# One value tile of an attention decode kernel loaded as its even rows and then eight 8-row transfers

## Chip, cores, metric

One core of one Trainium2 chip. The metric is device time in microseconds (us) of one execution. Repeats of the kernel before agree within 0.05%.

## The reference, cut to what matters

One decode step: layer norm, attention of 4 new tokens over a cache, output projection, residual, then a gated MLP with residual.

```python
B, Sq, D = 4, 1, 512;  H, Sk, Dh = 32, 8192, 128
scores = einsum("bhqd,bhkd->bhqk", q, k_cache) * Dh ** -0.5
p = softmax(scores);  o = einsum("bhqk,bhkd->bhqd", p, v_cache)
h = x + o.reshape(B, Sq, H * Dh) @ wo          # then h + MLP(layernorm(h))
```

k_cache and v_cache hold 268 MB each in bfloat16 and are read once; everything else is small. Loads are the whole cost.

## The kernel before

The cache passes through a ring of 4 buffers of 4 MiB, 128 partitions of 32 KiB. A tile is two heads of keys or of values; 64 tiles of each. SyncE issues every load, each as soon as the former tile in its buffer has been used. Row p of a tile (32 KiB, contiguous in HBM) goes to partition p.

```python
ring = SB("ring", [128, NS, TW], BF16)                     # NS = 4, TW = 16384
...
def kv_src(t, cache):                                      # [128 rows, 32 KiB each]
    h = 2 * t
    return cache[h // H, h % H:h % H + 2, :, :].rearrange("h (p r) d -> (h p) (r d)", p=64)
...
def load(it):
    kind, t = it
    slot = slot_of.get(it)
    ...                                                    # the last tiles are cut in pieces
    uses[slot] += 1
    sem, val = s_slot[slot], 16 * uses[slot]
    if kind == "k":
        dst, src = ringv(slot), kv_src(t, A_k_cache)
    elif kind == "v":
        dst, src = ringv(slot), kv_src(t, A_v_cache)
    ...
    return [(lambda e: e.dma_start(dst, src).then_inc(sem, 16), sem, val)]
```

VectorE transposes key tiles, TensorE makes scores and the products with the value tiles; both wait for the tile's semaphore. At the end a tail of pieces (output projection, MLP weights, last value tile) is issued, with the last two full tiles interleaved.

## Time and profile before

| | before |
|---|---|
| time, median | 1295.27 us (4 runs, 1295.11 to 1295.41) |
| DMA rate in the stream | 427 to 434 GB/s |
| key tile, issue to landing | 29.7 us |
| value tile, issue to landing | 33.9 us |
| VectorE busy | 636.9 us (49%) |
| TensorE matmul busy | 494.7 us (38%) |

The page of the kernel before: the DMA busy share and rate in 40 slices of the span, the packet counts, the queue, the chain that ended last, and two lines of the issues (count, KB each, us to landing). q1 is SyncE's queue, q8 and q14 fetch instructions.

```profile
DMA  9999999999999999999999999999999999999998
GB/s 405 432 428 433 433 427 433 431 430 434 427 431 432 429 431 432 432 428 433 432 430 429 433 429 431 431 432 431 431 429 432 431 429 434 430 430 431 428 382 322
DMA packets 26069, 551.46 MB, mean 426 GB/s; under 512 B 2340, under 2 KB 8232, under 8 KB 9256
...
q1 hardware_dynamic: 26016, 550.78, 99.5%
q8 instruction: 38, 0.62, 0.2%
q14 instruction: 7, 0.06, 0.0%
...
DMA 80%; PE 12%; SPq 4%; DVE 3%; issue 0%; ACT 0%
...
ring<-in_A_k_cache_dram SPq DMA_DIRECT2D x64, 4096.0 KB, 29.7
ring<-in_A_v_cache_dram SPq DMA_DIRECT2D x63, 4096.0 KB, 33.9
```

The DMA engines are busy throughout, and a tile takes 9.7 us of stream but lands 30 us or more after its issue: some three tiles always stand in the queue. No compute engine is near full. The kernel is bound by its 16 DMA engines.

Stages of the kernel before (us; then busy time and instruction count of TensorE matmuls, TensorE weight loads, VectorE, ScalarE and GpSimd; TensorE clock; DMA share; GB/s). The middle ones are those where the change will act.

```profile
600.00:690.00 90.00, 33.88 (x310) 11.78 (x314) 49.13 (x50) 3.67 (x6) 0.00 (x0) 0.58 1.00 431
692.00:696.00 4.00, 1.51 (x21) 0.41 (x20) 0.71 (x1) 2.61 (x5) 0.00 (x0) 0.93 1.05 451
698.00:718.00 20.00, 8.73 (x74) 3.88 (x74) 10.39 (x11) 0.00 (x0) 0.00 (x0) 0.59 1.01 432
730.00:830.00 100.00, 36.78 (x357) 12.88 (x349) 48.12 (x47) 3.67 (x6) 0.00 (x0) 0.61 1.00 430
```

In a stage of 4 us the rate is rough (451 GB/s; a packet of 32 KiB may count wholly in one stage); over 20 us it is 432 GB/s, as everywhere.

The trace also has a record of every DMA packet. It says nothing about which engine moved it, but each engine moves its packets back to back (eight of 1.216 us make the 9.72 us from one tile to the next), and each transfer ends with one 4-byte semaphore packet per engine that took part (16 for a whole tile, 4 for the 4-row load of x). So the finishing times of the 16 engines can be read tile by tile. Times of packets are counted here, as in the profile views, from the start of the span. A 32 KiB packet takes 1.216 us (median), eight per engine and tile. For the tile that ends from 720 us on:

```
before, 16 semaphore packets of one tile, us after the first at 720.8:
0 0.31 0.43 0.51 0.58 0.69 1.00 | 3.38 3.40 3.43 3.51 3.99 4.88 5.07 5.26 5.48
```

Seven engines are ahead of nine. The gaps come from instruction fetches, as the prediction tells: after a 16 KiB fetch one of the 16 finishing times moves back by about 1.55 us (at 593, 634 or 886 us, for example), after one of 8 KiB by 0.97 us.

### The profile page before, as it was taken

Reading aid. Unit: us, or ns where it says so; the run is one execution under the profiler, and the core shown is the slowest. Engines: PE = TensorE matmul, PEld = TensorE weight load, DVE = VectorE, ACT = ScalarE, POOL = GpSimd, SP = SyncE. Lnnn points to the kernel's source line nnn. Section 1 sums busy time; section 2 is a strip of 40 time slices with the busy share of each in tenths; the row PEclk is TensorE's granted clock in tenths of the full one; section 3 lists DMA queues with packets and bytes.
Section 4 is the critical chain, followed back from the end, with each engine's and each line's share of the span. In section 5 each row is a group of like instructions: output and inputs, shape, how many; then the busy total and the mean of one; then the engine's idle time right before and its main releaser. Section 6 shows DMA issues by size and latency. Waiting matters only on the chain.

```text
span 1293.4 us, 10805 instructions
## 1 busy us (share of the span) xinstructions
PE 494.7 (38%) x4867; PEld 183.3 (14%) x4867; DVE 636.9 (49%) x657; ACT 70.7 (5%) x118; POOL 10.7 (1%) x22
## 2 busy tenths in 40 slices
PE   2443334334234244334334334343343343343436
PEld 1011111111011011111111111011111111111114
DVE  5974644545545544635536545545545446445300
ACT  2010100001010010100101010010100101000010
POOL 3000000000000000000000000000000000000000
PEclk8556566566565565565565666665665655665665
DMA  9999999999999999999999999999999999999998
GB/s 405 432 428 433 433 427 433 431 430 434 427 431 432 429 431 432 432 428 433 432 430 429 433 429 431 431 432 431 431 429 432 431 429 434 430 430 431 428 382 322
DMA packets 26069, 551.46 MB, mean 426 GB/s; under 512 B 2340, under 2 KB 8232, under 8 KB 9256
## 3 DMA queue, kind: packets, MB, share of 16 engines
q1 hardware_dynamic: 26016, 550.78, 99.5%
q8 instruction: 38, 0.62, 0.2%
q14 instruction: 7, 0.06, 0.0%
q10 hardware_dynamic: 8, 0.00, 0.0%
HBM read 550.77 MB, written 0.00 MB: 426 GB/s over the span
## 4 chain that ended last, share of the span: by engine, by line
DMA 80%; PE 12%; SPq 4%; DVE 3%; issue 0%; ACT 0%
DMA ring<-in_A_v_cache_dram 76%; PE PS L441 7%; PE PS L417 4%; SPq L222 2%; DMA ring<-in_A_k_cache_dram 2%; DVE kT L399 2%; SPq L238 1%; DMA ring<-in_A_wq_dram 1%; DMA ring<-in_B_w_down_dram 1%; SPq L230 1%; SPq L258 0%; PE PS L332 0%; DVE Lq L376 0%; DVE ring L349 0%; PE PS L359 0%
## 5 line engine op out<-in xcount | busy, mean ns | idle before, releaser
L399 DVE STREAM_TRANSPOSE kT<-ring 128x1024 uint32<-128x1024 uint32 x512 | 587.9, 1209 | 480.9 <-DMA ring<-in_A_k_cache_dram 480.9
L417 PE MATMUL PS<-kT,Lq 128*32 128x512 bf16 x2048 | 241.3, 619 | 570.1 <-DVE kT L399 447.8
L441 PE MATMUL PS<-ring,PTz 128*32 128x512 bf16 x2048 | 215.6, 566 | 205.3 <-DMA ring<-in_A_v_cache_dram 205.3
L417 PEld LDWEIGHTS PS<-kT,Lq 128*32 128x32 bf16 x2048 | 69.0, 136 | 705.4 <-DVE kT L399 481.6
L441 PEld LDWEIGHTS PS<-ring,PTz 128*32 128x32 bf16 x2048 | 64.9, 128 | 323.2 <-DMA ring<-in_A_v_cache_dram 196.8
L476 ACT ACTIVATE negm<-PS 128x1 f32<-128x1 f32 x16 | 2.7, 171 | 1125.1 <-PE PS L472 1125.1
L502 DVE STREAM_TRANSPOSE Et<-Ep 128x512 bf16<-128x512 bf16 x16 | 11.4, 712 | 97.4 <-ACT Ep L498 97.4
L511 ACT ACTIVATE PTz<-Et 64x512 bf16<-64x512 bf16 x32 | 34.0, 1062 | 12.8 <-DVE Et L502 12.5
L516 DVE TENSOR_SCALAR Zs<-PS,rinv 128x512 f32<-128x512 f32 x16 | 11.6, 723 | 37.6 <-PE PS L441 37.6
L523 PE MATMUL PS<-SelZ,Zs 128*128 128x8 f32 x128 | 17.8, 265 | 0.9 <-DVE Zs L516 0.9
L523 PEld LDWEIGHTS PS<-SelZ,Zs 128*128 128x128 f32 x128 | 16.3, 200 | 9.9 <-issue 8.1
L455 DVE TENSOR_REDUCE mx<-PS 128x1 f32<-128x512 f32 x16 | 10.5, 657 | 3.9 <-PE PS L417 3.9
L478 ACT ACTIVATE E_sb<-PS,negm 128x512 bf16<-128x512 f32 x16 | 11.0, 688 | 0.7 <-ACT negm L476 0.2
L498 ACT ACTIVATE Ep<-PS 128x512 bf16<-128x512 f32 x16 | 9.6, 597 | 11.3 <-PE PS L494 11.3
L483 PEld LDWEIGHTS PS<-sig,Gsum 128*128 128x128 f32 x32 | 8.0, 313 | 13.4 <-issue 13.4
L483 PE MATMUL PS<-sig,Gsum 128*128 128x1 f32 x32 | 9.4, 363 | 0.0
L472 PEld LDWEIGHTS PS<-onesf,rowx 1*128 1x128 f32 x32 | 6.8, 265 | 12.5 <-issue 12.5
L472 PE MATMUL PS<-onesf,rowx 1*128 1x1 f32 x32 | 8.2, 323 | 0.0
L494 PE MATMUL PS<-E_sb,Sel 128*32 128x512 bf16 x64 | 7.0, 429 | 1.9 <-ACT E_sb L478 1.3
L349 DVE CAST ring<-PS 128x512 bf16<-128x512 f32 x4 | 2.5, 684 | 9.8 <-PE PS L332 9.8
L528 DVE CAST OT<-PS 128x8 bf16<-128x8 f32 x16 | 2.1, 132 | 9.6 <-PE PS L523 9.6
L332 PE MATMUL PS<-ring,xnT 128*32 128x512 bf16 x32 | 3.5, 615 | 6.6 <-DMA ring<-in_A_wq_dram 6.6
(80 smaller groups left out, 85.4 us busy)
## 6 DMA issues: line engine op xcount, KB each, us to landing
ring<-in_A_k_cache_dram SPq DMA_DIRECT2D x64, 4096.0 KB, 29.7
ring<-in_A_v_cache_dram SPq DMA_DIRECT2D x63, 4096.0 KB, 33.9
ring<-in_A_wq_dram SPq DMA_DIRECT2D x1, 4096.0 KB, 12.3
kT<-in_A_wo_dram SPq DMA_DIRECT2D x8, 512.0 KB, 17.3
ring<-in_A_v_cache_dram SPq DMA_DIRECT2D x1, 2048.0 KB, 18.6
ring<-in_A_v_cache_dram SPq DMA_DIRECT2D x2, 1024.0 KB, 18.2
ring<-in_B_w_gate_dram SPq DMA_DIRECT2D x1, 1792.0 KB, 20.0
ring<-in_B_w_up_dram SPq DMA_DIRECT2D x1, 1792.0 KB, 23.5
```

What stands on the lines that cost most here:

```text
L222: return [(lambda e: e.dma_start(wo_v[:, HW * t:HW * t + HW, :], A_wo.rearrange("(h p) f -> p h f", p=128)[:, HW * t:HW * t + HW, :]).then ...
L230: return e.dma_start(ringv(slot)[:, c0:c1], kv_src(t, A_v_cache)[:, c0:c1]).then_inc(s_piece[i], 16)
L238: return e.dma_start(wd_v[:, t0:t1, :], B_w_down.rearrange("(t p) f -> p t f", p=128)[:, t0:t1, :]).then_inc(s_piece[3 + i], 16)
L399: return e.transpose(kT[:, buf, i * q:(i + 1) * q].bitcast(U32), ringv(src)[:, base + i * q:base + (i + 1) * q].bitcast(U32))
L417: mm = e.matmul(bS[g % 2][32 * j:32 * (j + 1), :], Lq[:, l0:l0 + 32], rhs, start=(s % GS == 0 and v == 0), stop=(s % GS == GS - 1 and v == 3),
L441: mm = e.matmul(bO[g % 2][32 * rq:32 * (rq + 1), :], PTz[:, g % 2, l0:l0 + 32], ringv(slot)[:, r0 * 128:(r0 + 4) * 128], start=(s % GS == ...
L472: p2_of[g] = P("pe", lambda e: e.matmul(bX[:, 0:1], rowx[0:1, :], onesf[0:1, 0:1], start=True, stop=True), [d2b_of[g], c_ones])
L483: L_of[g] = P("pe", lambda e: e.matmul(bX[:, 0:1], Gsum[:, :], sig[:, 0:1], start=True, stop=True), [exp_of[g], a1_of[g], d_g])
L502: et_of[g] = P("dve", lambda e: e.transpose(Et[:, :], Ep[:, :]), [epc_of[g]] + list(ptc_of.get(g - 1, ())))
L511: return e.activation(dst, src, ACT.Copy)
L516: z_of[g] = P("dve", lambda e: e.tensor_scalar(Zs[:, :], bO[g % 2][:, :], rinv[:, g % 2:g % 2 + 1], None, op0=ALU.mult), [pv_of[g * GS + G ...
L523: mm = e.matmul(bX[:, 256:264], Zs[:, 128 * r:128 * (r + 1)], SelZ[:, r, :], start=(r == 0), stop=(r == 3))
```

## The change

Value tile 32 of 64, in the middle, is no longer loaded by one transfer of 128 rows but by nine: the 64 even rows, then 8 transfers of 8 rows that lie 16 apart (1, 17, ..., 113; then 3, 19, ...). The bytes, their places and the final semaphore count are the same. The name LOW8 suggests the intent, which the code does not state: it moves work to eight engines, presumably those that are ahead.

```diff
+        LOW8 = ("v", NT2 // 2)
+        LOW8_PARTS = [slice(0, 127, 2)] + [slice(p, p + 113, 16) for p in range(1, 16, 2)]
+
         def load(it):
             kind, t = it
             slot = slot_of.get(it)
+            if it == LOW8:
+                uses[slot] += len(LOW8_PARTS)
+                ops = []
+                for ps in LOW8_PARTS:
+                    def f(e, ps=ps, sem=s_slot[slot]):
+                        return e.dma_start(ring[ps, slot, :], kv_src(t, A_v_cache)[ps, :]).then_inc(sem, 16)
+                    ops.append((f, s_slot[slot], 16 * uses[slot]))
+                return ops
```

## The prediction

> **What bounds the kernel.** The DMA engines: the 40-slice table has their busy share at 9 in 39 slices, 427 to 434 GB/s until the tail; the stages view gives DMA 1.00 from 60 to 1180 us, VectorE about half. The chain of waits is 76% value-tile transfers. Tiles land about 30 us after issue (29.7 key, 33.9 value: the issue list), so some three tiles of 9.7 us stand in the queue.
>
> The trace's packet records say more. A 4 MiB tile is 128 packets of 32 KiB, median 1.216 us, back to back on 16 engines, 8 each. So the time is the packet sum of the engine furthest behind, and they are not level: for the tile landing near 700 us seven finish within 1.0 us, nine 3.3 to 5.5 us later; at the last key tile nine are 5.35 to 8.66 us behind. The cause is 16 KiB instruction fetches (36 records; about 1.06 us each and a slowed packet, about 1.55 us lost), which visit eight engines in turn; a ninth gets rarer 8 KiB fetches (about 0.97 us lost each) and ends 5.35 us behind.
>
> **What the change does.** Same bytes, same buffer, one tile of 128. The even rows, 64, put 4 packets on each of 16 engines. Each odd transfer has 8 rows. [...] The 4-row load of x has 4 data and 4 semaphore packets[...] +4 x 1.216 = +4.9 us low, -4.9 us high. Eight more semaphore packets per low engine (9 ns each): under 0.1 us. Eight more issues of 0.33 us: hidden by the queue. All waits use the final count.
>
> **On the critical path.** The low engines' surplus stays, since later tiles are balanced and the queue never runs dry. Its cost depends on which engines lag. My reading is that the eight fetch engines are the high half, so the change unloads laggards: they end at most 3.8 us behind instead of 8.66. Low engines end 5 to 6 us behind, but the ninth laggard would be low: 5.35+4.9=10.2. Net 0 to +1.5 us. If laggards are in the low half, the full +4.9. A further risk: [...] odd packets take up to double and the total could rise 10 to 20 us. No packet of this trace tests that.
>
> **Prediction:** 1297 us (+2 us, +0.15%); 80% range 1293 to 1309. Faster by over 2%: 0.005; within 2%: 0.97; slower by over 2%: 0.025.
>
> **What would show it.** 64 odd packets on eight engines near 700 us, of about 1.22 us [...]; the split tile landing 4 to 5 us later against its neighbours; afterwards the finishing spread within a tile changed by about 9.7 us between the halves, kept to the end; tail length, VectorE and TensorE busy times unchanged.
>
> **What would make it wrong.** Engines chosen by partition, not count (0 us); [...] the fast half being the low half without the ninth laggard (up to 3 us faster); gaps of a microsecond per transfer that the queue doesn't hide (+8 us).

The sum came to 0 to +1.5 us net, put as +2 us (1297 us). What stood before "+4 x 1.216" is the author's estimate, from the 4-row load with its 4 semaphore packets, that an 8-row transfer runs on 8 engines, so that eight engines ("low") carry 4+8=12 packets of this tile and the other eight ("high") 4, instead of 8 each. The risk of 10 to 20 us was named outside the sum; it stands as the author's guess.

## More of the kernel before

The chain of waits of the kernel before near the tile in question (start us, us, what):

```profile
672.92 0.02 issue
672.93 34.37 DMA ring<-in_A_v_cache_dram
707.30 0.14 issue
```

The waits for loads (us in total, times, longest us):

```profile
DVE kT L399 <- DMA ring<-in_A_k_cache_dram: 480.9, 60, 11.6
...
PE PS L441 <- DMA ring<-in_A_v_cache_dram: 205.3, 65, 10.5
```

A key tile comes every other tile, about every 19.4 us, and VectorE works about 9 us on it, so waits of some 10 us are normal (11.6 us is the longest); a disturbance of the stream must show as a longer one.

## The result

1310.97 us median of 4 runs (1310.35 to 1313.77), against 1295.27 us for the kernel before: 15.7 us slower. The ratio is 1.0125, 95% interval 1.0108 to 1.0143. Ratios here are the mean time of one kernel's fast runs over the mean of the other's in the same rounds, so not quite the ratio of the medians quoted. That is within 2%, but eight times the forecast +2 us and above the range (up to 1309). The profiled execution was the run of 1313.77 us, the slowest of the four; this matters for the tail below.

The page after:

```profile
DMA  9999999999999999999999999999999999999997
GB/s 405 430 431 432 431 431 431 432 430 432 431 431 431 431 430 431 431 433 430 431 430 273 410 432 431 431 432 432 431 430 431 430 431 431 431 431 432 398 367 303
DMA packets 26133, 551.46 MB, mean 420 GB/s; under 512 B 2404, under 2 KB 8296, under 8 KB 9320
...
q1 hardware_dynamic: 26080, 550.78, 99.2%
```

One slice has fallen to 273 GB/s and the next to 410, while the busy share above it still shows 9: the engines were busy but moved half as much. The packet count rose by 64, all of them tiny (under 512 B): the even rows have the 16 semaphore packets that the whole tile had before, and 8 more transfers have 8 each. So an odd transfer does run on 8 engines.

The same stages after:

```profile
600.00:690.00 90.00, 33.47 (x310) 11.77 (x314) 49.13 (x50) 3.66 (x6) 0.00 (x0) 0.58 1.00 431
692.00:696.00 4.00, 1.85 (x21) 0.63 (x21) 0.71 (x1) 2.27 (x5) 0.00 (x0) 0.86 1.05 451
698.00:718.00 20.00, 2.42 (x18) 0.95 (x18) 9.76 (x10) 0.00 (x0) 0.00 (x0) 0.50 0.99 214
730.00:830.00 100.00, 38.72 (x361) 14.09 (x353) 48.20 (x48) 3.67 (x6) 0.00 (x0) 0.60 1.00 430
```

The even rows, at about 691 to 696 us, still ran at full rate. The 20 us in which the odd transfers ran had 214 GB/s at a DMA share of 0.99. From 730 us on the rate is what it was.

The chain and the waits after (L231 is the new transfer's line; the value tile's matmuls are now L454, the key transposes L412):

```profile
678.22 0.56 SPq L231
678.78 0.05 issue
678.83 47.13 DMA ring<-in_A_v_cache_dram
725.96 0.14 issue
```

```profile
DVE kT L412 <- DMA ring<-in_A_k_cache_dram: 499.0, 60, 27.7
...
PE PS L454 <- DMA ring<-in_A_v_cache_dram: 226.6, 65, 21.1
```

The tile landed at 725.96 us instead of 707.30. The wait of VectorE for keys rose by 18.1 us, with one wait of 27.7 us instead of at most 11.6. Issuing cost nothing that mattered. All nine issues together took 5.98 us of the queue, more than the 0.33 us apiece that was predicted:

```profile
673.41 5.98 SPq L231 DMA_DIRECT2D ring<-in_A_v_cache_dram  x9
```

but that ended 12 us before the first packet of the tile was due. VectorE busy (636.6 us) and TensorE busy (494.1 us) are unchanged.

In the packet records of the profiled run, 192 packets of 32 KiB that started between 696 and 725 us took over 1.35 us ("slow" below), their median 2.40 us. Together they took 216 us more than at 1.216 us each. Over 16 engines this is 13.5 us: most of the loss. The tile has only 64 odd packets. The other two thirds of the slow packets are the neighbouring loads on the same and on the other eight engines: in this phase no engine was fast.

### The profile page after: what moved, and what is told of

It is laid out like the page before. It is cut to its first block, busy times and chain, and to the rows that moved or that the text cites. A ratio compares the mean times of both kernels' runs of the same rounds, so it can differ in the third digit from the quotient of the medians.

```text
span 1311.8 us, 10813 instructions
## 1 busy us (share of the span) xinstructions
PE 494.1 (38%) x4867; PEld 183.4 (14%) x4867; DVE 636.6 (49%) x657; ACT 70.7 (5%) x118; POOL 10.6 (1%) x22
## 4 chain that ended last, share of the span: by engine, by line
DMA 80%; PE 12%; SPq 5%; DVE 3%; issue 0%; ACT 0%
DMA ring<-in_A_v_cache_dram 76%; PE PS L454 7%; PE PS L430 4%; SPq L235 2%; DMA ring<-in_A_k_cache_dram 2%; DVE kT L412 2%; SPq L251 1%; DMA ring<-in_A_wq_dram 1%; DMA ring<-in_B_w_down_dram 1%; SPq L271 1%; SPq L231 0%; PE PS L345 0%; DVE Lq L389 0%; SPq L243 0%; DVE ring L362 0%
## 5 line engine op out<-in xcount | busy, mean ns | idle before, releaser
L412 DVE STREAM_TRANSPOSE kT<-ring 128x1024 uint32<-128x1024 uint32 x512 | 588.0, 1209 | 499.0 <-DMA ring<-in_A_k_cache_dram 499.0
L454 PE MATMUL PS<-ring,PTz 128*32 128x512 bf16 x2048 | 214.8, 564 | 226.6 <-DMA ring<-in_A_v_cache_dram 226.6
L454 PEld LDWEIGHTS PS<-ring,PTz 128*32 128x32 bf16 x2048 | 64.9, 128 | 344.9 <-DMA ring<-in_A_v_cache_dram 199.2
L529 DVE TENSOR_SCALAR Zs<-PS,rinv 128x512 f32<-128x512 f32 x16 | 11.6, 724 | 38.6 <-PE PS L454 38.6
```

The source lines that it names most:

```text
L412: return e.transpose(kT[:, buf, i * q:(i + 1) * q].bitcast(U32), ringv(src)[:, base + i * q:base + (i + 1) * q].bitcast(U32))
L454: mm = e.matmul(bO[g % 2][32 * rq:32 * (rq + 1), :], PTz[:, g % 2, l0:l0 + 32], ringv(slot)[:, r0 * 128:(r0 + 4) * 128], start=(s % GS == ...
L529: z_of[g] = P("dve", lambda e: e.tensor_scalar(Zs[:, :], bO[g % 2][:, :], rinv[:, g % 2:g % 2 + 1], None, op0=ALU.mult), [pv_of[g * GS + G ...
```

## The experiments

Most kernels below change only the list of row ranges of tile 32; "packets" are those of 32 KiB within some 30 us of it. Kernels that leave out or permute rows are wrong. The comparison with the reference called all of them correct nonetheless: one tile of 64 is too little for its tolerance, so that word says nothing about them.

The theories: **imbalance** (the sum of the prediction: only the count of packets per engine changed), **H** (HBM: rows at power-of-two distance hinder each other when read), **K** (8-row transfers, or many small ones, are slow in themselves), **P**, later **D** (the destination: engines that write certain partitions of SBUF at the same time slow each other). Which partitions these are was assumed before the runs; no trace names the engine or the way by which a partition is written. P and D stand only for what they forecast of each kernel: twice 1.216 us, 2.4 us a packet, where two engines get in each other's way, and four times, 4.9 us, for neighbouring rows.

### e1: even and odd halves, each on all 16 engines

```diff
-LOW8_PARTS = [slice(0, 127, 2)] + [slice(p, p + 113, 16) for p in range(1, 16, 2)]
+LOW8_PARTS = [slice(0, 127, 2), slice(1, 128, 2)]
```

> One part of the change alone: the tile as two 64-row transfers, even rows and odd rows, each over all 16 engines, no 8-row transfers. Theory P [...]: all 128 packets of the tile about 2.4 us, the two halves take 9.7 us instead of 4.9 us each, total +9 to +10 us. Theory H (the HBM source rows at a power-of-two stride alias): the same, +9 to +10 us. Theory K (the 8-row transfers themselves, 8 engines, are what is slow, and slow everybody): packets 1.22 us, total within 0.5 us of before.

Measured: 1295.14 us, ratio 0.9999 (0.9984 to 1.0014), no slow packets but single ones of about 1.7 us after fetches, as the kernel before has them too. Stage of e1 in which the two halves run:

```profile
698.00:702.00 4.00, 0.00 (x0) 0.00 (x0) 4.00 (x5) 0.00 (x0) 0.00 (x0) 0.50 1.03 442
```

Both P and H, as I had put them, expected +9 to +10 us and are off here. The even-row transfer of the change is innocent. K survives. If P is to hold, rows of stride 2 must be free of the slowing, against what I had assumed; how the rows of a transfer are dealt to the engines, no trace shows.

### e2: the same halves as blocks of 64 neighbours

```diff
+LOW8_PARTS = [slice(0, 64), slice(64, 128)]
```

> As the even and odd halves, but rows 0 to 63 and rows 64 to 127: contiguous in HBM, and in SBUF 64 neighbouring partitions. Theory P: [...] packets of about 2.4 us and +9 to +10 us, as for even and odd. Theory H: the source is as contiguous as the full tile's, packets 1.22 us, total within 0.5 us of before.

Measured: 1311.12 us, ratio 1.0119 (1.0102 to 1.0136): +15.8 us. Here every engine has 8 packets as before (a 64-row transfer showed 16 semaphore packets in the change), there is no 8-row transfer and the HBM source is as contiguous as ever.

```profile
693.00:699.00 6.00, 0.16 (x4) 0.00 (x0) 0.71 (x1) 2.72 (x3) 0.00 (x0) 0.90 1.02 213
```

213 GB/s with 16 engines busy is half the normal rate. This speaks for P, the destination, and against H, K and imbalance at once. The loss was larger than the 10 us expected, as the slow phase lasted beyond the tile's 128 packets (about 215 were slow): presumably while the late engines finish the second half, early ones already write the next tile (the 16 finishing times of a tile are up to 5.48 us apart here in the kernel before).

### e3 and e4: destination and source apart

e3 keeps the change's destinations and reads plain blocks of rows; e4 is the reverse. Both are wrong (rows of one tile permuted).

```diff
+LOW8_SRC = [slice(0, 64)] + [slice(64 + 8 * j, 72 + 8 * j) for j in range(8)]     # e3; e4 swaps the lists
-    return e.dma_start(ring[ps, slot, :], kv_src(t, A_v_cache)[ps, :]).then_inc(sem, 16)
+    return e.dma_start(ring[ps, slot, :], kv_src(t, A_v_cache)[qs, :]).then_inc(sem, 16)
```

> The change with its SBUF destinations kept (even rows, then 8 transfers of 8 partitions 16 apart) but plain sources: rows 0 to 63, then 8 consecutive rows each. Wrong result on purpose (rows of one value tile permuted). Theory P: as the change, +14 to +17 us, packets about 2.4 us and 217 GB/s while it lasts. Theory H: packets 1.22 us; only the engine imbalance is left, total 0 to +2 us.

Measured e3: 1313.96 us, ratio 1.0139 (1.0124 to 1.0154): +18.6 us, a little above the +14 to +17 expected; 189 slow packets, against 192 of the change. Both kernels have single runs near 1311 and near 1314 us (three of four near 1314 here, one of four in the change), so the 3 us between their medians say little. Stage of e3 in the odd phase:

```profile
698.00:702.00 4.00, 0.00 (x0) 0.00 (x0) 4.00 (x4) 0.00 (x0) 0.00 (x0) 0.50 0.93 205
```

> The reverse: the change's HBM sources (even rows, then rows 16 apart), into plain destinations: partitions 0 to 63, then 8 consecutive partitions each. Wrong result on purpose. Theory H: as the change, +14 to +17 us, packets about 2.4 us. Theory P: first half 2.4 us a packet; [...] these packets take about 4.9 us and the total is worse than the change, +30 us or more.

Measured e4: 1323.96 us, ratio 1.0222 (1.0206 to 1.0237): +28.6 us. In its first part the packets took about 2.5 us, in its second mostly 3.3 us.

The source does not matter (e3: 205 GB/s with plain sources), the destination does: H is out. e4's direction fits P, its size does not quite: I had expected 4.9 us a packet for transfers of eight neighbouring rows and +30 us or more.

### f1 to f4: which partitions belong together

After e1, a rival to D's choice of rows seemed possible, **C**: that an engine's own partitions are 8 neighbours (8i to 8i+7). It explains e1 and e2 too. f2 and f3 are twins: both load only rows 0 to 63, by 8 transfers of 8 rows on 8 engines, and differ only in the distance of the rows (upper rows left out, wrong). f1 loads the full tile by 8 transfers that use all 16 engines.

```diff
+LOW8_PARTS = [slice(o, 128, 8) for o in range(8)]                                             # f1
+LOW8_PARTS = [slice(o, 64, 8) for o in range(8)]                                              # f2
+LOW8_PARTS = [slice(b + p, b + p + 29, 4) for b in (0, 32) for p in range(4)]                 # f3
```

> The tile as 8 transfers of 16 rows, 8 apart, so as many small transfers as the change has, but each over all 16 engines. Theory C (an engine's own partitions are 8 neighbours, engine i has 8i to 8i+7, and everybody slows when an engine writes into another engine's eight): every row falls to its owner, packets 1.22 us, total within 0.7 us of before. Theory D [...] packets about 2.4 us, +9 to +16 us. Theory K (many small transfers cost in themselves): also slower.

Measured f1: 1310.74 us, ratio 1.0118 (1.0103 to 1.0133), 208 slow packets. Its stage:

```profile
698.00:702.00 4.00, 0.00 (x0) 0.00 (x0) 0.00 (x0) 0.00 (x0) 0.00 (x0) 0.50 0.94 188
```

> Only rows 0 to 63 of the tile are loaded (wrong result on purpose; the upper rows keep what the buffer held), as 8 transfers of 8 rows, 8 apart, on 8 engines each. Theory C: row 8i+o goes to engine i, its owner: packets 1.22 us; low engines keep their 8 packets, high ones lose 8 (9.7 us); the finish is then set by the ninth laggard, which is a low engine 5.35 us behind where the last was 8.66: total 2.5 to 4 us faster. Theory D: [...] packets about 2.4 us, +8 us or more. Theory K (8-engine transfers are slow in themselves): packets 2.4 us.

Measured f2: 1304.30 us, ratio 1.0070 (1.0055 to 1.0085): +9.1 us with half of the tile left out; 159 slow packets. Its stage:

```profile
693.00:699.00 6.00, 0.00 (x0) 0.00 (x0) 0.71 (x1) 2.72 (x3) 0.00 (x0) 0.89 1.02 208
```

> The same rows 0 to 63 by 8 transfers of 8 rows on 8 engines, but the rows of one transfer are 4 apart (wrong result on purpose). Theory D: [...] packets 1.22 us and 2.5 to 4 us faster than before. Theory C: engines write into others' eights, two engines to an owner: packets about 2.4 us for all 16 engines while it lasts, total +5 to +13 us.

Measured f3: 1295.01 us, ratio 0.9995 (0.9980 to 1.0010), no slow packet but those after fetches. Its stages:

```profile
691.00:694.00 3.00, 2.26 (x30) 0.73 (x22) 0.00 (x0) 1.54 (x4) 0.00 (x0) 0.92 0.99 426
698.00:702.00 4.00, 0.00 (x0) 0.00 (x0) 4.00 (x4) 0.00 (x0) 0.00 (x0) 0.50 0.99 426
```

C falls in all three, and D's forecasts of the rates hold: rows 4 apart ran at 426 GB/s, rows 8 apart at 208 (f2) and 188 (f1); why, no trace shows. f3 is also the clean test of K: eight 8-engine transfers in a row ran at full rate while the other eight engines skipped the tile. The imbalance that this leaves between the engines slows no packet either.

Who took the eight transfers can be read from the trace's records of semaphores: each ring buffer has its own, raised about 0.44 us after an engine's semaphore packet, so the 16 finishing times of one tile can be told from those of its neighbours. Eight engines raise tile 32's semaphore eight times in a row, 1.22 us apart, right after they finish the tile before: five of the seven leaders and three of the nine behind. The others, two leaders and six of the nine, finish the next tile 9.72 us after the tile before, so they skipped tile 32. This is that next tile:

```
semaphore raised by the 16 engines, us after 702.35
before: 9.21 9.54 9.73 9.73 9.79 9.92 10.21 | 12.64 12.65 12.70 12.71 13.15 14.05 14.28 14.46 14.68
f3:     0 0.03 | 2.91 3.13 3.19 3.22 4.88 5.00 | 9.22 9.51 9.88 9.89 10.31 | 12.75 14.38 14.43
```

So the prediction's reading that the eight fetch engines are the other half holds for six of them at most: three of the nine that lag (12.75, 14.38 and 14.43 in f3's line) take the 8-row transfers. Below, the eight engines that take them are called low, the others high. f3 gained only 0.2 us in the median (one of its four runs, not the profiled one, was 1293.23 us) and not the 2.5 to 4 us expected, for two reasons. At a late full tile, finished at 1225.2 us in the kernel before, the mean engine was 4.8 us earlier (the 64 packets left out, over 16), but the last engine, a low one that skipped nothing, only 1.75 us. The tail gave that back: 66.1 us from there to the end of the MLP weights instead of 64.5. Stage of the tail, before and then f3:

```profile
1236.00:1246.00 10.00, 3.60 (x36) 1.77 (x28) 0.17 (x1) 0.00 (x0) 0.00 (x0) 0.67 0.87 345
```

```profile
1236.00:1246.00 10.00, 2.29 (x20) 1.37 (x12) 0.17 (x1) 0.00 (x0) 0.00 (x0) 0.67 0.58 212
```

In the tail the queue issues transfers of hundreds of short packets (512 of 1 KiB in a load of wo), and a single issue can take over 10 us there (12.12 us in the kernel before, from 1220.11 us on); the DMA share falls to 0.87 and, in f3, 0.58, so engines stand idle. What the issue waits for was not shown.

f4 was meant as a smaller dose of the change, with two 16-apart transfers:

```diff
+LOW8_PARTS = [slice(0, 127, 2)] + [slice(o, 128, 8) for o in (3, 5, 7)] + [slice(1, 128, 16), slice(9, 128, 16)]
```

> A smaller dose of the change: even rows at once, odd rows 8 apart over 16 engines except for two transfers of 8 rows 16 apart, as the change has eight. Theory C: the slow phase lasts while those two are written, from the first engine's entry to the last one's end, 7 to 12 us at half rate: total +3 to +7 us, packets about 2.4 us in it. If the loss were a fixed cost of the odd transfers' start, it would be +14 us as before; if there were no slowing but only imbalance, within 1 us.

Measured: 1303.27 us, ratio 1.0061 (1.0044 to 1.0078): +8.1 us, 135 slow packets. The design was bad. It took 8-apart rows for harmless filler, by C; f1 shows that they are slow too. So f4 measures no dose and only agrees that fewer such rows cost less.

### g1: the change with rows 4 apart

```diff
+LOW8_PARTS = [slice(0, 127, 2)] + [slice(b + p, b + p + 29, 4) for b in (0, 32, 64, 96) for p in (1, 3)]
```

> The change with one number altered: the 8 rows of an odd transfer are 4 apart instead of 16, so the packets of each engine are those of the change. Theory D [...]: the first four transfers (rows below 64) [...] 1.22 us; the last four (rows 64 and up) [...] packets about 2.4 us on all 16 engines for 10 to 14 us. Total +6 to +10 us against before, about half of the change's loss. If only the count of 8-row transfers mattered, +15 us as the change.

Measured: 1309.31 us, ratio 1.0107 (1.0092 to 1.0122): +13.8 us; 134 slow packets. By their semaphore packets the leading ones of the eight engines run the first four odd transfers from about 697 to 702 us, 1.22 us each, and the last four from then on, about 2.5 us each. Two stages of g1, the first mostly of that fast phase, the second wholly of the slow one:

```profile
695.00:700.00 5.00, 0.00 (x0) 0.00 (x0) 2.54 (x3) 1.85 (x2) 0.00 (x0) 0.51 1.02 439
703.00:713.00 10.00, 1.55 (x14) 0.63 (x6) 4.29 (x6) 0.00 (x0) 0.00 (x0) 0.50 1.00 211
```

The pattern is the one that D forecast: full rate with rows below 64 (439 GB/s), half rate with rows of the upper half (211 GB/s), on the same eight engines. Why the half matters was not shown. The time missed the range expected (+6 to +10). The slow packets make 9.1 us over 16 engines, and at the late tile used for f3 the mean engine was 9.2 us late. But the last engine was 12.7 us late there, as one that lags is among the eight with 12 packets, and the tail took 1.1 us more.

### g3: eight neighbours at once

```diff
+LOW8_PARTS = [slice(8 * j, 8 * j + 8) for j in range(8)]                  # rows 0 to 63 only, as f2 and f3
```

> Rows 0 to 63 by 8 transfers of 8 consecutive rows on 8 engines (wrong result on purpose, upper rows skipped), to be read beside the same rows 4 apart [...] and 8 apart [...]. Theory D: [...] packets up to 4.9 us, total slower than the 8-apart kernel by 8 us or more, +17 us or more against before. If the cost were a fixed halving [...]: packets 2.4 us and about +9 us as with 8 apart.

Measured: 1304.93 us, ratio 1.0072 (1.0055 to 1.0089): +9.5 us. Packets took mostly 2.1 to 2.8 us on all engines, about as with 8 apart.

```profile
693.00:699.00 6.00, 0.83 (x12) 0.16 (x4) 0.71 (x1) 2.72 (x3) 0.00 (x0) 0.78 1.08 229
```

This is the other branch of what was expected. So eight neighbouring rows did not cost twice what rows 8 apart cost (229 against 208 GB/s in the same stage); the estimate of 4.9 us a packet fails here. The engines are up to 5 us apart at this point, so they are not all in the same transfer. This may be why; no run separates it.

### g2, h1, h2: do the other engines slow too?

In the change only eight engines ran the odd transfers, yet all sixteen slowed (192 slow packets, 64 of them odd). g2 loads eight upper rows one at a time, so one engine at a time; h1 and h2 use four engines (all wrong: rows left out). The two branches expected of each are that only the engines slow that get in each other's way (the "sharers"), or that everybody slows; the assumptions about who these are, are cut.

```diff
+LOW8_PARTS = [slice(0, 127, 2), slice(1, 128, 4)] + [slice(p, p + 1) for p in (67, 99, 71, 103, 75, 107, 79, 111)]   # g2
+LOW8_PARTS = [slice(c, c + 4) for c in (16, 20, 24, 28)]                                                              # h1
+LOW8_PARTS = [slice(c, c + 13, 4) for c in (16, 17, 18, 19)]                                                          # h2
```

> One look for the packets; wrong result on purpose (8 upper rows not loaded). Even rows and rows 1+4i over 16 engines, then 8 transfers of one row each[...] at most 2 engines have packets of about 2.4 us, the other 14 stay at 1.22 us, DMA rate above 380 GB/s. If it slows everybody: all engines' packets go to about 2.4 us and the rate falls to about 217 GB/s while it lasts.

> One look for the packets; wrong result on purpose (only rows 16 to 31 of the tile are loaded). Four transfers of 4 consecutive rows on 4 engines: [...] If sharing hurts only the sharers: 4 engines with packets of 4.9 us or more, [...] rate above 320 GB/s. [...] all 16 at 2 us or more and the rate under 260 GB/s while it lasts.

> One look; the same rows 16 to 31 by four transfers of 4 rows 4 apart on 4 engines: [...] If sharing hurts only the sharers: 8 engines at about 2.4 us, 8 at 1.22 us, rate about 320 GB/s. [...] all 16 near 2.4 us and about 217 GB/s.

The times of these (1303.17, 1297.82 and 1294.76 us) are of no interest, as rows are missing. The stages, of g2, h1 and h2 in this order:

```profile
700.00:714.00 14.00, 2.41 (x18) 0.94 (x18) 7.26 (x8) 0.00 (x0) 0.00 (x0) 0.50 1.00 389
```

```profile
693.00:699.00 6.00, 0.57 (x12) 0.07 (x4) 0.71 (x1) 2.72 (x3) 0.00 (x0) 0.78 0.92 137
```

```profile
693.00:699.00 6.00, 0.00 (x0) 0.00 (x0) 0.71 (x1) 2.46 (x3) 0.00 (x0) 0.85 1.01 208
```

Packets by the time of their start, from the packet records:

```
g2, 701 to 703 us: 23 packets of 1.215 to 1.234 us, 2 of 2.49 to 2.51 us
h2, 695 to 697 us: 12 packets, all 2.53 to 2.56 us
h1, 693 to 695 us: 8 packets, all 3.46 to 3.77 us
```

With one row at a time (g2) two packets at a time are slow, at twice 1.22 us, presumably that row's and one other engine's; the others mostly stay between 1.22 and 1.40 us, so they lose little. With four engines (h1, h2) every packet that starts in these stretches is slow by about the same factor, although at most four at a time are of tile 32. So one engine slows few, and from somewhere between one and four engines on it holds up everybody (each of the three kernels was run once). By what mechanism was not shown.

## Why the prediction was wrong

- **Right:** the bound (DMA engines, the latest engine decides); 8 engines to an 8-row transfer (64 new semaphore packets); the sum of packets per engine. At the late tile used for f3 the low eight moved about 9.5 us against the high eight where 9.7 was predicted (an estimate, with the places of the halves before taken from f3). Right too: the hidden issues, the unchanged compute engines.
- **Wrong, and the failing step:** "+4 x 1.216 = +4.9 us low, -4.9 us high" and the net "0 to +1.5 us" took every packet at 1.216 us. The odd packets and everything beside them took 2.40 us (median). The prediction named this as "a further risk", put at 10 to 20 us, which is what came, but kept it out of the point and cut the range at 1309. The mis-sized term is this one: 0 in the sum, 13.5 us measured (excess of 192 slow packets over 16 engines). Experiments e2, f2 against f3, and g1 show that it depends on which partitions the engines write at the same time; e3 that it is not the source; f3 that it is neither the 8-engine transfer nor the imbalance. Why these partitions was not shown, but theory D foretold which kernels slow down in f1, f2, f3 and g1, and the rival grouping C failed in the first three.
- **Wrong too, but smaller:** "the eight fetch engines are the high half, so the change unloads laggards". Three of the nine engines that lag are in the low half (f3), so the change loads some of them further: the branch "if laggards are in the low half, the full +4.9" was nearer. It cost up to 3.4 us in the profiled run (below).
- **Even as a risk it was put too narrowly:** "odd packets take up to double". All engines' packets doubled, here (192 slow packets, of which the tile's odd rows are 64) and in h2, where 4 engines load tile 32 (12 packets of 2.53 to 2.56 us).
- **The even rows** did not suffer (e1, 1295.14 us), which the prediction had not asked.
- **The remainder:** in the profiled run the span is 18.4 us longer. At the late tile used for f3 the mean engine was 13.5 us late, which is the slow packets, and the last engine 16.9 us; the 3.4 us between them are mostly the imbalance, against the predicted 0 to +1.5 (in e2 and f1, where every engine keeps 8 packets, this difference is 0.9 and 0.8 us). The tail, predicted unchanged, took 65.9 us instead of 64.5. That run is 2.8 us above the median, so how the 15.7 us of the median split is not known. The tail took 65.6 to 66.1 us in the change, e3, f3 and g1, and 64.0 to 64.9 us in the other timed kernels, e4, f2 and g3 with their 8-engine transfers among them; why is open.
- **Could the idea win at all?** Not shown; the argument against it rested on an assumption about partitions that no run tests. No full-tile version here beat the kernel before. Two kernels tie with it, e1 and f3, and f3 leaves out rows.
- **Open:** why some rows slow each other and others do not; why e4, h1 and g3, with transfers of neighbouring rows, slow by about 2.7, 2.8 to 3.1 and 1.8; at which number of engines the common slowing begins; what the tail's issues wait for.

## What to carry to other kernels

When a stream already runs the DMA engines at full rate (431 GB/s at a share of 1.00), cut a tile only in row patterns that were measured at that rate: here strides of 2 over all 128 rows (442 GB/s in a stage of 4 us), or transfers of 8 rows 4 apart within rows 0 to 63 (426), were free, while two blocks of 64 (213), rows 8 apart (208 and 188), rows 16 apart (214), and 8 rows 4 apart in the upper half (g1, 211) halved the rate of all engines for as long as they ran. A busy share of 1.00 at half the GB/s (0.99 at 214 in the change) is the sign of it; look at the durations of equal packets, not at the share. And when a named risk costs ten times the expected effect and nothing in the trace speaks against it, it belongs in the range.
